# Scores of two attention pieces in one TensorE burst, five PSUM banks as one stock, and the first third in fixed sequences

## The chip, the cores and the metric

The kernel runs on one core of a Trainium2 chip. The time is that of the device from start to end, in microseconds. Engines: PE (TensorE, matrix products), DVE (VectorE), ACT (ScalarE), POOL (GpSimd) and SP, whose queue issues nearly all DMAs. PE writes its results to PSUM, which has eight banks of 128 x 512 f32.

## The reference

Attention with two kinds of masks, and behind it one feed-forward layer over all tokens. q and k are scaled by 7.3, so the scores are not small; all is f32.

```python
B, H, S, D = 8, 8, 576, 64                     # q, k, v: (B, H, S, D)
scores = q @ k.T / sqrt(D)
mask   = (0 <= i - j < 32)                     # heads 0 to 3, "local"
mask   = (i >= j) and (i % 32 == j % 32)       # heads 4 to 7, "strided"
attn   = softmax(where(mask, scores, -1e9))
x      = (attn @ v).transpose(0, 2, 1, 3).reshape(4608, 512)
h      = x @ w_in                              # 512 -> 2048
g      = h * erf(softplus(h))
out    = g @ w_out                             # 2048 -> 512
```

## The kernel before

**Feed-forward.** The 4608 tokens go in 12 chunks of 384, the 2048 hidden units in 16 slices of 128. One slice of one chunk is an f-tile; there are 192. An f-tile is a first-product group on PE (`mm1`, L814: twelve products of 128 x 384 into one PSUM bank, `h`; x and the weights are each split into a high and a low part, and three of the four combinations are summed), nine steps on ACT and DVE (L822, L819, L843, L846, L849: four tanh and products that stand for h * erf(softplus(h)), then the split into `ghi` and `glo`), and three second-product groups (`mm2`, L877: three products of 128 x 512 for each of three token tiles, summed over the slices in the banks `o0` to `o2`). The bank of `h` is free when `glo` is written. `a`, `ghi` and `glo` have two buffers each.

**Attention.** Each batch has six pieces: three thirds of the queries for the local heads (True) and three for the strided ones (False). The 12 pieces of batches 0 and 1, needed by the first chunks, are done by `head` with masks added on PE. The other 36 are done by `quad`: 32 score products of 64 x 64 (L559) into two banks (`ps`), then for each bank the mask on DVE (L574, a minimum, which also copies to SBUF and so frees the bank), the maximum on POOL (L580), subtraction on DVE (L587), exponential on ACT (L594) and the sum on POOL (L600), then DVE steps that bring the reciprocal sums into place. Two pieces share one `products` step: 64 value products (L665) into two `ps` banks, which are scaled in place (L696) and split into `xhi` (L717, ACT) and `xlo` (L722, DVE); with `xlo` the bank is free. A burst is a run of such 64 x 64 products between the 128 x 128 products of the f-tiles.

**PSUM before.** Three banks for `h` (pool `ps_h`, also for the transposes and some scores of the heads), two for `ps`, three for `o`.

**Weights.** 32 blocks of w_in and w_out come as pairs of 32-bit words (L760), are turned into f32 by three DVE steps (L766, L773, L779), and split by ACT and DVE (L784, L787). All that falls in the first third, where the loads of 16.8 MB of words, the heads and the first chunks compete.

**Order.** A planner (`Plan`) simulates the engines with a cost for each operation and picks, engine by engine, the ready operation of the smallest key; its result is the program order of each engine. Keys come from tables (`WK`, `HK`, `GK`, `AK`, `FT` ...) and, for the 1087 operations that it names, from the list `ORDER`. Ahead of the first f-tile, the planner fills PE's free time with products that nobody reads (`warm`, L1057).

The lines around which the change turns:

```python
s = [buf("ps_ps", "ps", [P, 512], f"s{i}_{pid}") for i in range(2)]     # quad
ph = buf("ps_h", "h", [P, 512], f"h_{k}")                               # ftile
px = [buf("ps_ps", "ps", [P, 512], f"x{p}_...") for p in range(2)]      # products
o_s = add("pe", 0.75, key, scores, [lq, *o_con, *last], [*s, *sm], [qk])
```

Of the kernel before, what the change touches and what calls it, by code (L numbers as in the profile page):

```python
# [32 lines left out]
WK = (-129.247, -1893.58, 98.5168, -2129.18, 127.551, 563.302, -1058.31, 207.105, 1224.65, 1267.83, 776.969, 2769.39, 1905.64, 459.073, 1076.72, 1052.12, -571.504, 270.885, -541.703, 359.21, 614.965, 583.382, 626.232, 272.891, 1466.2, 1009.72, -1281.88, 2826.45, 1224.64, 459.156, 1917.17, -1415.81)  # L33
LD = (226.738, 72.4203, -180.254)
HD = (-336.803, 299.919, 1136.27, 1085.87, -1250.39, 1255.86, -283.893, -2829.06, -1852.42, -715.65, -833.303, -831.384)
HK = (-211.98, -3338.2, -1501.79, -1392.83, 143.38, -60.2353, 220.878, 315.727, 281.824, 331.969, 646.928, 824.11)
GK = (69.7483, 204.571, -202.002, -12.5924, 109.465, 414.462, 58.9581, 1.10569, -170.147, -56.9842, 70.5204, -218.953, 0.416193, 310.64, 101.626, 128.829, -366.195, -122.429, 227.847, 32.916, 114.694, -116.251, -133.254, 189.13, 397.368, -138.217, 135.932, -37.9147, -43.0676, 44.7781, 229.201, 144.855, -268.989, -169.213, 72.314, 185.886)
QD = (-79.5815, -82.8971, -2.37199, 155.063, -3.45178)
ADT = -0.840127
CK = 40.0  # L40
AK = (77.4271, 192.803, -60.2978, 41.0326, 70.3192, 185.174, -70.7401, 2.22243, -109.704, 315.813, -26.4327, -155.795, 62.5451, 236.782, 72.0876, 265.805, 176.553, 8.32189)
PF = 26.1751
# [32 lines left out]
class Buf:  # L75


    def __init__(self, tag, make):
        self.tag, self.make, self.users = tag, make, []
        self.tile = None  # L80
# [29 lines left out]


class Op:
    def __init__(self, eng, dur, key, emit, after, new, use, earliest):
        self.eng, self.dur, self.key, self.emit, self.earliest = eng, dur, key, emit, earliest
        self.after, self.new = list(after), list(new)
        self.start = self.end = None
        self.behind = []
        self.locks = eng == "pool" or eng == "dve" and emit.__name__ in TWO
        for b in self.new + list(use):
            b.users.append(self)  # L120


class Plan:

    ENGINES = ("pe", "act", "dve", "pool", "sp")
    SAME = {"pe": 0.0, "act": 0.14, "dve": 0.13, "pool": 0.1, "sp": 0.0}
    LATENCY = {"pe": 0.25, "act": 0.2, "dve": 0.15, "pool": 0.6, "sp": 0.1}  # L130
    PATIENCE = 0.002
    ENTER = 0.08
# [12 lines left out]
    def _ready(self, op, live):  # L145
        t = op.earliest
        if any(p.end is None for p in op.behind):
            return None
        for p in op.after:
            if p.end is None:  # L150
                return None
            t = max(t, p.end + (self.SAME if p.eng == op.eng else self.LATENCY)[op.eng])
        for i, b in enumerate(op.new):
            order = live.setdefault(b.tag, [])
            n = len(order) - self.bufs[b.tag] + sum(x.tag == b.tag for x in op.new[:i])
            if n >= 0:
                for u in order[n].users:
                    if u.end is None:
                        return None
                    t = max(t, u.end + (self.SAME if u.eng == op.eng else self.LATENCY)[op.eng])  # L160
        return t

    def order(self):
        queue = {e: sorted((o for o in self.ops if o.eng == e), key=lambda o: o.key) for e in self.ENGINES}
        free = dict.fromkeys(self.ENGINES, 0.0)
        live, dma, left = {}, self.RAMP[0], len(self.ops)
        cold = None
        held = {"dve": 0.0, "pool": 0.0}
        entered = False
        while left:  # L170
            best = None
            for e in self.ENGINES:
                can = [(o, n, self._ready(o, live)) for n, o in enumerate(queue[e][: self.WINDOW])]
                floor = max(free[e], dma - BACKLOG) if e == "sp" else free[e]
                port = held.get({"dve": "pool", "pool": "dve"}.get(e), 0.0)
                can = [(max(t, floor, port if o.locks else 0.0), o.key, e, n) for o, n, t in can if t is not None]
                if e == "pe" and self.filler and self.filler[0].end is not None:
                    can.append((max(free[e], self.filler[0].end + 0.2), 1e9, e, -1))
                if can:
                    soon = min(can)[0] + self.PATIENCE  # L180
                    c = min((key, t, e, n) for t, key, e, n in can if t <= soon)
                    if best is None or c[1] < best[0]:
                        best = (c[1], c[0], c[2], c[3])
# [3 lines left out]
            if n < 0:  # L187
                o = Op(e, 0.11, 0.0, self.filler[1], (), (), (self.filler[2],), 0.0)
                self.ops.append(o)
                left += 1  # L190
            else:
                o = queue[e].pop(n)
            if self.filler and o is self.filler[3]:
                self.filler = None
            o.start = t
            if e == "sp":
                free[e] = t + 0.6
                was, dma = dma, max(dma, t + 0.6) + o.dur
                dma += self.RAMP[1] if was < 3.0 <= dma else 0.0
                o.end = dma + 1.5  # L200
# [18 lines left out]
def attention_moe(  # L219
# [58 lines left out]
    def dve(n, x=1.0):  # L278
        return 0.067 + n * x / 960.0
# [935 lines left out]
```

## Time and profile before

| | us |
|---|---|
| runs shown, median (lowest to highest) of 3 | 918.6 (918.18 to 918.61) |
| profiled execution | 918.11 |
| its span, first to last instruction | 916.3 |
| PE, DVE, ACT, POOL busy | 906.4, 691.9, 574.4, 317.4 |
| PE's share of the chain that ended last | 81% |

A busy engine is one that has an instruction in flight; the products of PE overlap, so its busy time contains what one product waits for the one before. The price of a piece of PE's work is therefore read from start to start in the timeline. Idle time is what ends a wait that nothing covered. What is off the chain costs nothing as long as it stays covered.

### The profile page before, as it was taken

To read this page: it belongs to the slowest core of one execution; us is meant where nothing else is said; L and a number is where in the kernel's file an instruction comes from. 1 tells how busy PE (TensorE), PEld (TensorE's weight loads), DVE (VectorE), ACT (ScalarE), POOL (GpSimd) and SP (SyncE) were. 2 spreads that over 40 slices of the span, in tenths; PEclk is the share of its full clock that TensorE was granted. 3 is DMA by queue.
4 is the path that set the end of the run, shared out by engine and by line. 5 is a ranking of instruction groups with operands and counts; after the bars stand their busy time and mean duration, and the time that the engine had idled before them with its cause. 6 is when DMAs were issued, how large, how long until landed. Compare 5 with 4: busy or idle time off the path is not lost.

```text
span 916.3 us, 18195 instructions
## 1 busy us (share of the span) xinstructions
PE 906.4 (99%) x7066; PEld 805.6 (88%) x7066; DVE 691.9 (76%) x1507; ACT 574.4 (63%) x1291; POOL 317.4 (35%) x170
## 2 busy tenths in 40 slices
PE   9999999999999999999999999999999999999998
PEld 6888989998888888899888888888899888999997
DVE  6999999757978888856887876788875767575553
ACT  5777677656556666566666566566656656655654
POOL 4521011304457445404455641644650323030000
PEclk9999999999999999999999999999999999999999
DMA  9972121013322122102221211212200300000000
GB/s 364 403 298 95 47 75 47 12 35 99 116 76 75 39 62 79 44 1 74 65 64 59 62 38 32 91 41 64 80 19 1 97 1 24 35 2 1 35 1 35
DMA packets 26726, 66.11 MB, mean 72 GB/s; under 512 B 2960, under 2 KB 3728, under 8 KB 26640
## 3 DMA queue, kind: packets, MB, share of 16 engines
q1 hardware_dynamic: 26496, 64.73, 20.5%
q8 instruction: 55, 0.90, 0.4%
q14 instruction: 31, 0.25, 0.1%
q10 hardware_dynamic: 144, 0.23, 0.1%
HBM read 53.15 MB, written 11.80 MB: 71 GB/s over the span
## 4 chain that ended last, share of the span: by engine, by line
PE 81%; DVE 11%; POOL 3%; ACT 2%; issue 2%; DMA 0%; SPq 0%; DVEq 0%; POOLq 0%; ACTq 0%
PE h L814 37%; PE o L877 36%; DVE a L819 2%; PE ps L559 2%; POOL su_True L600 2%; PE ps L665 1%; ACT a L822 1%; PE warm L1057 1%; POOL su_False L600 1%; DVE glo L849 1%; DVE ps L696 1%; PE av L450 1%; DVE h L843 1%; DVE xlo L722 1%; DVE sm L367 1%
## 5 line engine op out<-in xcount | busy, mean ns | idle before, releaser
L877 PE MATMUL o<-pair,ghi 128*128 128x512 f32 x1154 | 359.1, 392 | 0.0
L822 ACT ACTIVATE a<-a 128x384 f32<-128x384 f32 x576 | 294.0, 523 | 103.2 <-DVE a L819 96.9
L819 DVE SCALAR_TENSOR_TENSOR a<-a,h 128x384 f32<-128x384 f32 x384 | 209.8, 547 | 135.0 <-ACT a L822 132.1
L814 PE MATMUL h<-xhi,pair 128*128 128x384 f32 x1536 | 302.7, 339 | 2.2 <-DVE glo L849 1.8
L814 PEld LDWEIGHTS h<-xhi,pair 128*128 128x128 f32 x1536 | 268.6, 188 | 14.5 <-DVE glo L849 5.9
L877 PEld LDWEIGHTS o<-pair,ghi 128*128 128x128 f32 x1154 | 212.4, 188 | 36.4
L877 PE MATMUL o<-pair,glo 128*128 128x512 f32 x577 | 224.6, 389 | 0.0
L822 ACT ACTIVATE a<-h 128x384 f32<-128x384 f32 x192 | 94.2, 491 | 142.1 <-PE h L814 141.4
L814 PE MATMUL h<-xlo,pair 128*128 128x384 f32 x768 | 164.4, 336 | 0.0
L843 DVE TENSOR_TENSOR h<-a,h 128x384 f32<-128x384 f32 x192 | 106.4, 556 | 44.2 <-ACT a L822 43.4
L814 PEld LDWEIGHTS h<-xlo,pair 128*128 128x128 f32 x768 | 136.0, 188 | 0.0
L877 PEld LDWEIGHTS o<-pair,glo 128*128 128x128 f32 x577 | 108.3, 188 | 23.1
L580 POOL PARTITION_ALL_REDUCE mx_False<-sm_False x36 | 51.5, 1466 | 203.8 <-DVE sm_False L574 190.9
L849 DVE TENSOR_TENSOR glo<-h,ghi 128x384 fp32r<-128x384 f32 x192 | 105.2, 548 | 11.4 <-ACT ghi L846 7.9
L580 POOL PARTITION_ALL_REDUCE mx_True<-sm_True x36 | 51.5, 1467 | 175.5 <-DVE sm_True L574 137.2
L846 ACT CAST ghi<-h 128x384 fp32r<-128x384 f32 x192 | 90.9, 473 | 33.4 <-PE o L877 27.9
L600 POOL PARTITION_ALL_REDUCE su_True<-sm_True x36 | 90.5, 2552 | 49.7 <-ACT ob L919 33.6
L600 POOL PARTITION_ALL_REDUCE su_False<-sm_False x36 | 91.1, 2562 | 11.0 <-ACT a L822 2.4
L360 POOL PARTITION_ALL_REDUCE mx<-sm x22 | 34.7, 1584 | 58.5 <-DVE w L766 21.3
L717 ACT CAST xhi<-ps 128x128 fp32r<-128x128 f32 (+3 forms) x72 | 21.4, 321 | 17.5 <-DVE ps L696 13.7
L594 ACT ACTIVATE sm_False<-sm_False 128x432 f32<-128x432 f32 (+1 forms) x36 | 18.7, 524 | 12.5 <-DVE sm_False L587 12.3
L610 DVE STREAM_TRANSPOSE tt_False<-su_False 64x448 f32<-64x448 f32 (+1 forms) x36 | 21.0, 583 | 5.2 <-POOL su_False L600 2.4
(83 smaller groups left out, 617.9 us busy)
## 6 DMA issues: line engine op xcount, KB each, us to landing
out<-ob SPq DMA_DIRECT2D x35, 256.0 KB, 2.0
words<-w_in SPq DMA_DIRECT2D x16, 512.0 KB, 7.9
words<-w_out SPq DMA_DIRECT2D x16, 512.0 KB, 7.5
qk_True<-qk_loc SPq DMA_DIRECT2D x18, 416.0 KB, 3.2
qk_False<-qk_str SPq DMA_DIRECT2D x12, 472.0 KB, 3.2
v_True<-v_all SPq DMA_DIRECT2D x18, 260.0 KB, 3.7
v_False<-v_all SPq DMA_DIRECT2D x18, 260.0 KB, 3.5
v<-v_all SPq DMA_DIRECT2D x10, 260.0 KB, 7.6
```

Source lines behind the costliest of these rows:

```text
L360: yield nc.gpsimd.partition_all_reduce(mx[:, :cols], sm[k][:, :cols], P, ReduceOp.max)
L580: yield nc.gpsimd.partition_all_reduce(mx[k][:, :cols], sm[k][:, :cols], P, ReduceOp.max)
L600: yield nc.gpsimd.partition_all_reduce(su[k][:, :cols], sm[k][:, :cols], P, ReduceOp.add)
L610: yield nc.vector.transpose(tt[rows, :width], t[rows, :width])
L717: yield nc.scalar.copy(hi, src)
L814: yield nc.tensor.matmul(ph[:, :CH], win[4 * s + cc][:, w, fs], x[cc // 2][:, cc % 2, c0 : c0 + CH], start=(i == 0), stop=(i == len(terms) ...
L819: yield nc.vector.scalar_tensor_tensor(out=out, in0=in0, scalar=scalar, in1=in1, op0=op0, op1=op1)
L822: yield nc.scalar.activation(dst, src, func, bias=bias[i], scale=scale)
L843: yield nc.vector.tensor_tensor(out=ph[:, :CH], in0=a.tile, in1=ph[:, :CH], op=ALU.mult)
L846: yield nc.scalar.copy(ghi.tile, ph[:, :CH])
L849: yield nc.vector.tensor_tensor(out=glo.tile, in0=ph[:, :CH], in1=ghi.tile.bitcast(F32), op=ALU.subtract)
L877: yield nc.tensor.matmul(po[:, half], g[:, ts], wout[f][:, w, half], start=(f == fs0 and i == 0), stop=(f == fs1 and i == 2 and half.stop ...
```

## The change

1. `quad` no longer issues its scores. A new function `attend` takes two pieces and issues their 64 score products as one PE step, which needs the four score banks of both at once; `softmax` holds the steps behind it as they were. There are 18 such bursts instead of 36.
2. The pools `ps_h` and `ps_ps` become one stock of five banks for `h`, score, value and transpose tiles. The planner picks the bank that has been free longest, and a step starts in its plan only when as many banks as it needs are vacant. Five banks are cleared at the start instead of two.
3. In the plan, score and value steps are put 0.5 us behind the moment at which they could start (`SLACK`), and the costs of loads are changed (first data at 3.05 us, 395 GB/s, landing 0.8 us).
4. Operations named in `ORDER` keep exactly that sequence on their engine (`strict`), SP's excepted; so do all first-product groups and score bursts. `ORDER` has new contents and names 1400 operations instead of 1087, up to about the 60th f-tile; the other tables of keys are new too.

```diff
-LD = (226.738, 72.4203, -180.254)
+LD = (-455.947, -13.8716, -393.415)
-QD = (-79.5815, -82.8971, -2.37199, 155.063, -3.45178)
+QD = (-172.068, -5.26238, -82.1718, 124.272, 198.844)
...
+SHARED, NBANK = {"ps", "s", "t", "h"}, 5
...
-    RAMP = 0.9, 1.4
+    BEGIN, LANDING = 3.05, 0.8
+    SLACK = {"scores": 0.5, "av": 0.5, "mm1": 0.0}
...
-        return t
+        need = sum(b.tag in SHARED for b in op.new)
+        if need:
+            free = sorted(self._vacant(op.eng))
+            if len(free) < need:
+                return None
+            t = max(t, free[need - 1][0])
+        return t + op.slack
+
+    def _vacant(self, eng):
+        out = []
+        for n, b in enumerate(self.held):
+            if b is None:
+                out.append((0.0, n))
+            elif all(u.end is not None for u in b.users):
+                out.append((max(u.end + (self.SAME if u.eng == eng else self.LATENCY)[eng] for u in b.users), n))
+        return out
...
-                can = [(o, n, self._ready(o, live)) for n, o in enumerate(queue[e][: self.WINDOW])]
+                can = [(o, n, self._ready(o, live)) for n, o in enumerate(queue[e][: self.WINDOW]) if not o.strict or o is turn[e][0]]
...
+            vacant = sorted(self._vacant(o.eng)) if any(b.tag in SHARED for b in o.new) else []
             for b in o.new:
                 live[b.tag].append(b)
+                if b.tag in SHARED:
+                    b.bank = vacant.pop(0)[1]
+                    self.held[b.bank] = b
...
-    banks = [ps_a.tile([P, 512], F32, name=f"ps{i}") for i in range(2)]
+    banks = [ps_a.tile([P, 512], F32, name=f"ps{i}") for i in range(NBANK)]
...
-        o_s = add("pe", 0.75, key, scores, [lq, *o_con, *last], [*s, *sm], [qk])
-        o_s.behind.extend(order_t)
...
+    def attend(pair, key, dt, last):
+
+        def scores():
+            for g in pair:
+                yield from g.scores()
+
+        o_s = plan.add(
+            "pe", 1.21, key, scores, [g.lq for g in pair] + [*o_con, *last],
+            [x for g in pair for x in (*g.s, *g.sm)], [g.qk for g in pair],
+        )
+        o_s.behind.extend(order_t)
+        o_s.slack, o_s.strict = plan.SLACK["scores"], True
+        for m, g in enumerate(pair):
+            softmax(g, o_s, key + 0.3 * m, dt)
+        return o_s
...
-        ph = buf("ps_h", "h", [P, 512], f"h_{k}")
+        ph = buf("ps", "h", [P, 512], f"h_{k}")
...
-    for i in range(2):
-        z = buf("ps_ps", "ps", [P, 512], f"clear{i}")
-        plan.add("dve", 0.4, -20.0 + i, clear(z), [], [z])
+    for i in range(NBANK):
+        z = buf("ps", "ps" if i < 4 else "s", [P, 512], f"clear{i}")
+        plan.add("dve", 0.4, -20.0 + 0.1 * i, clear(z), [], [z])
...
     for n, i in enumerate(ORDER):
         plan.ops[i].key = n - 10000.0
+        plan.ops[i].strict |= plan.ops[i].eng != "sp"
```

The order on PE, in the seventh chunk, before: the scores of the second and third strided piece of batch 5 (`qk_5_False_1`, `qk_5_False_2`; `o0_6` is a bank of the chunk's output, `h_101` the bank of f-tile 101). Sixteen rows stand for the 32 products of a piece, twelve for a first-product group.

```order
L877 MATMUL o0_6_0_5974<-pair17_311,ghi_97_5978 128x512 x2
L877 MATMUL o0_6_0_5974<-pair17_311,glo_97_5987 128x512
L559 MATMUL ps1_90<-qk_5_False_1_5734 64x54
L559 MATMUL ps0_89<-qk_5_False_1_5734 64x54
...
L814 MATMUL h_101_6093<-xhi0_81,pair4_1163 128x384
...
L559 MATMUL ps1_90<-qk_5_False_2_5778 64x36
L559 MATMUL ps0_89<-qk_5_False_2_5778 64x36
...
L877 MATMUL o1_6_0_5981<-pair17_311,ghi_97_5978 128x512 x2
```

The same two pieces on PE now; `ps0` to `ps4` are the five banks of the stock.

```order
L923 MATMUL o0_6_0_5762<-pair24_1554,ghi_104_6121 128x512 x2
L923 MATMUL o0_6_0_5762<-pair24_1554,glo_104_6129 128x512
L582 MATMUL ps3_89<-qk_5_False_1_5850 64x54
L582 MATMUL ps4_90<-qk_5_False_1_5850 64x54
...
L582 MATMUL ps2_88<-qk_5_False_2_5865 64x36
L582 MATMUL ps0_86<-qk_5_False_2_5865 64x36
...
L923 MATMUL o1_6_0_5771<-pair24_1554,ghi_104_6121 128x512 x2
...
L858 MATMUL ps1_87<-xhi0_78,pair8_1679 128x384
...
L858 MATMUL ps3_89<-xhi0_78,pair8_1679 128x384
...
L858 MATMUL ps4_90<-xhi0_78,pair12_1233 128x384
```

The two score bursts, which had a first-product group between them, are one that takes four banks; one second-product group and three first-product groups follow, into the fifth bank and into two banks of the burst.

The start of DVE's order before (`cap`, `con`, `ident` and `neg` are constants, `w32_2` is weight block 2).

```order
L1060 MEMSET cap_86 128x150
L974 MEMSET ps0_89 128x512
L974 MEMSET ps1_90 128x512
L959 CAST con_85<-con_f_91 128x446
L960 COPY ident_88<-con_f_91 128x128
L963 TENSOR_SCALAR neg_87<-con_f_91 128x128
```

The start of DVE's order now, and further down the fourth clear with its neighbours.

```order
L1106 MEMSET cap_83 128x150
L1005 CAST con_82<-con_f_91 128x446
L1006 COPY ident_85<-con_f_91 128x128
L1020 MEMSET ps0_86 128x512
L1020 MEMSET ps1_87 128x512
L1009 TENSOR_SCALAR neg_84<-con_f_91 128x128
...
L1020 MEMSET ps4_90 128x512
...
L1020 MEMSET ps3_89 128x512
```

The clears have moved behind the constants, three stand in the first ten rows, and two are among the work of the heads.

## Rows read from the trace of the kernel before

**Rows 1.** The page: span, busy times by engine, shares of the chain by engine.
```profile
span 916.3 us, 18195 instructions
PE 906.4 (99%) x7066; PEld 805.6 (88%) x7066; DVE 691.9 (76%) x1507; ACT 574.4 (63%) x1291; POOL 317.4 (35%) x170
PE 81%; DVE 11%; POOL 3%; ACT 2%; issue 2%; DMA 0%; SPq 0%; DVEq 0%; POOLq 0%; ACTq 0%
```
**Rows 2.** Busy time by stretch: length, five engines, granted clock, DMA share, GB/s.
```profile
0.00:25.00 25.00, 23.00 (x268) 17.37 (x269) 15.89 (x34) 14.12 (x37) 11.19 (x11) 1.00 0.95 366
25.00:50.00 25.00, 25.00 (x288) 21.68 (x286) 24.12 (x57) 18.71 (x58) 13.37 (x9) 1.00 1.03 405
...
45.60:107.40 61.80, 60.47 (x442) 54.28 (x441) 60.69 (x142) 43.74 (x95) 12.45 (x9) 1.00 0.45 164
107.40:912.70 805.30, 802.33 (x6102) 716.63 (x6101) 595.12 (x1288) 500.06 (x1108) 282.52 (x144) 1.00 0.15 47
331.00:359.10 28.10, 27.82 (x256) 24.54 (x255) 22.39 (x52) 18.12 (x43) 15.66 (x8) 1.00 0.25 78
```
**Rows 3.** The chain that ended last, in order of time: start, length, what.
```profile
6.57 2.51 PE warm L1057 x23
...
885.96 4.17 PE h L814 x24
890.12 4.08 PE o L877 x18
...
904.53 8.21 PE o L877 x39
```
**Rows 4.** Timeline of PE: start, length, line, operation, out<-in, count, [idle].
```profile
209.44 1.16 PE L665 MATMUL ps<-sm_True,v_True 64*64 64x64 f32 x64
210.53 1.67 PE L814 MATMUL h<-xhi,pair 128*128 128x384 f32 x8
...
303.45 1.55 PE L814 MATMUL h<-xhi,pair 128*128 128x384 f32 x8
...
305.63 0.69 PE L559 MATMUL ps<-qk_False 64*64 64x54 f32 x32
306.24 1.67 PE L814 MATMUL h<-xhi,pair 128*128 128x384 f32 x8
...
308.54 0.67 PE L559 MATMUL ps<-qk_False 64*64 64x36 f32 x32
309.14 0.73 PE L877 MATMUL o<-pair,ghi 128*128 128x512 f32 x2
...
313.35 1.55 PE L814 MATMUL h<-xhi,pair 128*128 128x384 f32 x8
```
**Rows 5.** Waits of PE's weight loads from 100 us on: total, times, longest.
```profile
PEld h L814 <- DVE glo L849: 5.2, 12, 0.7
PEld ps L559 <- DVE xlo L722: 4.3, 9, 0.8
```
**Rows 6.** Timeline of DVE, ACT and PE at the start and around the first f-tile.
```profile
1.11 1.03 DVE L974 MEMSET ps<- 128x512 f32 x2
...
39.67 0.68 DVE L787 TENSOR_TENSOR pair<-w,pair 128x512 fp32r<-128x512 f32 x1
...
44.23 0.26 ACT L389 CAST xhi<-t 128x144 fp32r<-128x144 f32 x1
...
44.52 0.31 DVE L394 TENSOR_TENSOR xlo<-t,xhi 128x144 fp32r<-128x144 f32 x1 [0.29 <-ACT xhi L389]
...
45.60 1.65 PE L814 MATMUL h<-xhi,pair 128*128 128x384 f32 x8
47.09 0.86 PE L814 MATMUL h<-xlo,pair 128*128 128x384 f32 x4
...
52.98 0.76 PE L328 MATMUL ps<-qk 128*128 128x144 f32 x4 [0.87 <-DVE xn L476]
```
**Rows 7.** Groups by line: the mask, count, busy time, mean ns, idle before.
```profile
L574 DVE TENSOR_TENSOR sm_True<-ps,cap 128x384 f32<-128x384 f32 x36 | 18.5, 549 | 0.5 <-PE ps L559 0.2
```

More of the change, by code (lines that the diff above doesn't have):

```diff
@@ L79, in __init__ @@
         self.tag, self.make, self.users = tag, make, []
-        self.tile = None
+        self.tile = self.bank = None
     def __getitem__(self, key):
@@ L169, in order @@
         entered = False
+        turn = {e: [o for o in queue[e] if o.strict] for e in self.ENGINES}
         while left:
@@ L240, in attention_moe @@
     ps_a = ctx.enter_context(tc.tile_pool(name="ps_a", bufs=1, space=PSUM))
-    ps_h = ctx.enter_context(tc.tile_pool(name="ps_h", bufs=3, space=PSUM))
     ps_o = ctx.enter_context(tc.tile_pool(name="ps_o", bufs=1, space=PSUM))
@@ L282, in act, with group @@
         return fixed + n / 1200.0
-    def group(b, loc, j, bank="ps", spare=None):
+    def group(b, loc, j, spare=None):
         g = SimpleNamespace()
@@ L305, in group @@
             sm, sm_b = [Part(both, i) for i in range(nbank)], [both]
-        s = [buf("ps_" + bank, bank, [P, 512], f"s{i}_{pid}") for i in range(nbank)]
-        pt = buf("ps_h", "h", [P, 512], f"t_{pid}")
+        s = [buf("ps", "s", [P, 512], f"s{i}_{pid}") for i in range(nbank)]
+        pt = buf("ps", "t", [P, 512], f"t_{pid}")
         def place(i, blk, h):
@@ L404, in loads, with head @@
         return lq, lv
-    def head(b, loc, j, key, dt, early, bank, num, sub_pe_too, norm_act):
+    def head(b, loc, j, key, dt, early, num, sub_pe_too, norm_act):
         spare = num if num < 6 else None
-        g = group(b, loc, j, bank, spare)
+        g = group(b, loc, j, spare)
         sm_b = g.sm_b
@@ L415, in head @@
         mx = [Part(mx_b, i) for i in range(nbank)]
-        pav = [buf("ps_o" if early else "ps_ps", f"o{i}" if early else "ps", [P, 512], f"av{i}_{pid}") for i in range(2)]
+        pav = [buf("ps_o" if early else "ps", f"o{i}" if early else "ps", [P, 512], f"av{i}_{pid}") for i in range(2)]
         xn_b = [buf("apool", "tt", [P, 512], f"xn{i}_{pid}") for i in range(2)]
@@ L535, in quad @@
         v = buf("zpool", "v", [P, 2 * WV], f"v_{pid}")
-        s = [buf("ps_ps", "ps", [P, 512], f"s{i}_{pid}") for i in range(2)]
+        s = [buf("ps", "ps", [P, 512], f"s{i}_{pid}") for i in range(2)]
         sm = [buf("apool", "sm", [P, 512], f"sm{i}_{pid}") for i in range(2)]
@@ L633, in quad, with softmax @@
         order_q[:], order_v[:] = [lq], [lv]
-        o_s = add("pe", 0.75, key, scores, [lq, *o_con, *last], [*s, *sm], [qk])
-        o_s.behind.extend(order_t)
+        done = [[], []]
+        return SimpleNamespace(**{k: x for k, x in locals().items() if k != "add"})
+    def softmax(g, o_s, key, dt):
+        s, sm, mx, su, tt, rc, cols, width = g.s, g.sm, g.mx, g.su, g.tt, g.rc, g.cols, g.width
+        mask, maxi, sub, exp, total, gather, invert, spread = g.mask, g.maxi, g.sub, g.exp, g.total, g.gather, g.invert, g.spread
+        add = plan.add
         o_e = []
@@ L857, in ftile @@
         first = add("pe", 2.08, v0, mm1, ready[0] + mm1_first[-1:], [ph])
+        first.strict = True
+        first.slack = plan.SLACK["mm1"] if pos else 0.0
         o = add("act", tp, at(FT[0]), n1, [first], [a], [ph])
@@ L1025, in chunks_of @@
         return [1] if (loc and j == 0) else ([2] if loc else [1, 2])
-    quads = []
+    quads, last = [], []
     for b in range(B):
@@ L1032, in attention_moe @@
                 n = 6 * b + i
-                done = head(b, loc, j, HK[n], HD[n], b == 0, "ps" if b or i % 2 else "h", n, SUB_PE[n], NORM_ACT[n])
+                done = head(b, loc, j, HK[n], HD[n], b == 0, n, SUB_PE[n], NORM_ACT[n])
                 for c in to:
@@ L1037, in attention_moe @@
                 k = 6 * b + i - 12
-                a = quad(
-                    b, loc, j, PRO + SLOT * GK[k], ADT * SLOT, PRO + SLOT * AK[k // 2] + k % 2, [quads[-1][0].o_s] if quads else []
-                )
+                a = quad(b, loc, j, PRO + SLOT * AK[k // 2] + 0.1 * (k % 2))
                 quads.append((a, b // 2, to))
                 if k % 2:
-                    products((quads[-2][0], quads[-1][0]), PRO + SLOT * AK[k // 2], ADT * SLOT)
+                    pair = (quads[-2][0], a)
+                    last = [attend(pair, PRO + SLOT * GK[k // 2], ADT * SLOT, last)]
+                    products(pair, PRO + SLOT * AK[k // 2], ADT * SLOT)
     for a, p2, to in quads:
```

58 lines of the change are left out of this document (30 added, 28 removed).

## The prediction, made before the changed kernel ran

> **What bounds the kernel now.** I read the page's totals first, then the busy times by stretch, then the chain that ended last, then TensorE's timeline at single places and the waits. The profiled execution took 918.11 us, of which 916.3 us are the span; the median of the three runs shown is 918.6 us, 0.5 us above. The sum below is made against 918.11. PE is busy 906.4 us of the span and carries 81% of the chain; DVE has 11% of it [rows 1]. By stretch, DVE is full from 25 to 107 us (24.12 of 25.00 and 60.69 of 61.80 us), and the DMA engines are full up to 50 us. After that PE is full: from 107.40 to 912.70 us it is idle for 805.30 - 802.33 = 3.0 us, at granted clock 1.00, while DVE has 210 us to spare [rows 2]. So a gain must come from work that PE no longer does, from PE's waits, or from the start before the first f-tile at 45.60 us [rows 6].
>
> What PE does behind 107.40 us can be counted. Where nothing disturbs it, 24 first products take 4.17 us, that is 2.08 us per f-tile, and 18 second products 4.08 us, that is 0.68 us per token tile and 2.04 us per f-tile [rows 3]. By the order of before, 180 first-product groups (375 us) and 545 second-product groups (371 us) stand behind this point, with 36 score bursts of 0.62 us and 18 value bursts of 1.09 us (42 us) [rows 4]. Together 788 us. The stretch has 805.3, so 17.5 us are something else: the price of going in and out of a burst, and waits.
>
> The price of a burst can be read where none waits. A first-product group ahead of a burst starts it after 305.63 - 303.45 = 2.18 us instead of 2.08; the group between two bursts takes 308.54 - 306.24 = 2.30 us; the six second products behind take 313.35 - 309.14 = 4.21 us instead of 4.08 [rows 4]. So two bursts cost 0.10 + 0.22 + 0.13 = 0.45 us beside their own products, 0.22 us each. I use 0.21. Fifty-four bursts make 11.3 us. What is left, some 6 us, are waits: 3.0 us of visible idle time and what PE loses when it starts up again. By name they are waits for glo (a bank of h that is not yet free) and for xlo (a bank of ps that is not yet free) [rows 5].
>
> **The change part by part.**
>
> Scores of two pieces in one burst. The order shows 18 score bursts of 64 products in place of 36 of 32, with the same products. Eighteen entries and exits go: 18 x 0.21 = **-3.8 us**. No row of before shows two pieces' scores back to back, so the seam between them is bounded: at 0.21 us the merge saves nothing, at 0 it saves all. The nearest row is the value burst, which runs the 64 products of two pieces in 210.53 - 209.44 = 1.09 us, 17 ns each [rows 4], with no seam of that size. I take 0.
>
> Five banks as one stock. Before, h has three banks and attention two; now a paired burst takes four of the five at once, so at most one f-tile may hold a bank when it starts. The order puts a long run of second products ahead of each burst and three first-product groups behind it. The first of the three uses the fifth bank, the next two use banks of the burst, and they need them only after two groups of work (0.68 and 2.08 us). DVE frees a bank with one mask of 0.55 us [rows 7], and the first piece's masks can run during the second piece's products, so this is covered unless DVE comes 1.5 us late. If that cover is gone, PE waits at the second or third group. In a dense stretch the order gives an f-tile some nine us of other PE work between its two products, so a late glo hurts less than before. What the burst waits for is the release of the last f-tiles' banks and of the two banks of the value products of the pair before: glo and xlo, the waits of rows 5. Before, the bursts' weight loads stood 4.3 us for xlo in nine places, at most 0.8 us; the first products' loads 5.2 us for glo in twelve [rows 5]. The planner now leaves 0.5 us ahead of every score and value burst, about the mean of these nine waits (0.48). Ends: all 6 us of waits go (-6), or every one of the 18 bursts stands 0.8 us (14.4 - 4.3 = +10). Behind a waiting burst stand three first products, and behind these ACT and DVE run dry, so such a wait is not made up. I take **-2 us**, about half of the waits on xlo.
>
> DVE's share of this: the pieces' operations are the same in number. A dense stretch of before, with one pair and six f-tiles, has DVE busy 22.39 of 28.10 us and GpSimd 15.66 [rows 2]. The new order's densest stretches also have six f-tiles from burst to burst. DVE stays under PE there; its queue is in order, so single hold-ups of one 0.55 us operation remain possible.
>
> The first third in fixed sequences. All engines get new orders up to about the 60th f-tile; what can cost or give more than a wait lies at the start, where DVE and the DMAs are full. PE's fillers ahead of the first f-tile fall from 135 to 123; 23 of them take 2.51 us, 0.109 us each [rows 3], so twelve are 1.3 us. This counts only if the data come earlier too. The data of the first group in before: the last xhi piece ends at 44.23 + 0.26 = 44.49 us, its xlo at 44.83, and the group starts at 45.60 us and reads xlo 1.49 us later [rows 6]. So there are 1.1 us of margin on xhi. Against it: five clears of banks on DVE instead of two, 0.52 us each [rows 6]. Three stand in the first ten rows, where DVE is idle 9.1 of 25 us [rows 2]; the two others fall where DVE is full and add 1.0 us ahead of the first group's last operand. The first group also needs the second weight block (w1), which DVE finished at 39.67 + 0.68 = 40.35 us in before [rows 6]. On SP's queue one weight block and one q/k piece more and one v piece less stand ahead of it now, 0.67 MB, 1.7 us at 405 GB/s [rows 2], and on DVE's queue some 4 us more work (an estimate: its order's operations by their mean times); so it is ready at about 44.2 us, where 45.60 - 1.3 = 44.3 would want it. Ends: -1.3 and +1.0. I take **-0.7 us**: the margin of 1.1 us carries the clears, and what is missing for the full 1.3 I leave out, since both operands come only just in time. Behind the first group the order interrupts the f-tiles for head work 13 times instead of 11, 2 x 0.2 = **+0.4 us**. The tail behind the last second product, which ends at 904.53 + 8.21 = 912.74 us [rows 3], has the same operations as before.
>
> Sum: 918.1 - 3.8 - 2.0 - 0.7 + 0.4 = **912.0 us**.
>
> **The rivals.**
>
> First: the start does not give, and the waits stay. DVE fills the stretch from 25 to 107 us [rows 2], the two clears and the shifted weights delay the first f-tile by 1.0 us, and bank waits of the new kind replace the old ones one for one. 918.1 - 3.8 + 1.0 + 0.4 = 915.7 us. For it: DVE is the bound there. Against it: the margin of 1.1 us [rows 6].
>
> Second: the waits go altogether, since the f-tiles have nine or more us between their two products where a tile's own chain is nine steps on ACT and DVE of about the 0.55 us of rows 7, some 5 us. 918.1 - 3.8 - 6 - 0.7 + 0.4 = 908.0 us. Against it: with two ghi and two glo buffers a tile's last steps still wait for second products two tiles before.
>
> Third, on the other side: the burst's four banks. In a dense stretch the chain of a pair (four masks, eight GpSimd reductions that keep it busy 15.66 of 28.10 us [rows 2], then gather, scale, hi, lo) ends shortly before the next burst needs its banks. Before, a burst needed two banks, now four at once, and it comes once instead of in two parts. If each of the 18 bursts stands 0.8 us, the longest that rows 5 shows, the time is 918.1 - 3.8 - 0.7 + 0.4 + 10.1 = 924 us. It decides from (3.4 + 0.7 + 4.3) / 18 = 0.47 us per burst on, where the gains are used up. Against it: the planner's 0.5 us of margin, and that such waits now come up in nine places of 36 only.
>
> Fourth: the price of a burst is paid per piece and not per burst, so that the merge saves nothing: 912.0 + 3.8 = 915.8 us. Against it: the value bursts [rows 4].
>
> Fifth: PE's waits become regular and its clock falls to the lower level, 1.2 GHz, in the dense stretches. Ten f-tiles at half speed would cost 41 us, 953 us. Against it: the granted clock is 1.00 in every stretch of rows 2, also in the one with PE's longest idle time behind the start, 0.87 us at 52.98 us [rows 6]. The Trainium skill, "TensorE: Matmul & The Clock Gate", section "A second HAM failure mode: psum-queue depth-cycling", tells of a kernel that cycled through PSUM banks and idled PE between groups of products, so that the clock swung between its two levels; a shared stock of banks is the place for it. By that rule this rival would decide; the trace of before, with two small stocks that are cycled as hard, shows no such swing.
>
> **How the numbers follow.** Forecast 912.0 with its own range of 909.5 to 915: 0.58. First rival 0.14, second 0.12, third 0.10, fourth 0.05, fifth 0.01. Two runs of this kernel can be told apart from about 0.2% (1.8 us) on: faster is below 916.8 here, slower above 920.4. Faster: 0.58 + 0.12, most of the first (0.10) and 0.02 of the fourth: 0.82. Slower: most of the third (0.08) and the fifth: 0.09. The same: the rest, 0.09. The range of 8 in 10 leaves out the deepest part of the second case and most of the third: 907.5 to 918.
>
> **What would show it.** Right: 18 score bursts of about 1.25 us, each with one surcharge; the first first-product group before 45.6 us; PE's waits on xlo and glo behind 107 us smaller in sum; granted clock 1.00. The stretch behind the first f-tile shorter by 4 to 6 us. Wrong: score bursts that wait for xlo or glo in most of 18 places, a seam inside the burst, a first f-tile after 46 us, or PE idle for more than the 61.80 - 60.47 = 1.3 us of before between 45.60 and 107.40 us [rows 2].

## The result and the profile after

The changed kernel takes 909.62 us (median of 4 runs, 909.1 to 910.02) against 918.51 us for the kernel before on the same chip (4 runs, 918.18 to 918.61): a ratio of 0.9904 with a 95% interval of 0.9886 to 0.9921. The forecast was 912.0 us, with 907.5 to 918.0 as its range. The profiled execution has a span of 907.4 us, 8.9 us less than the 916.3 of [rows 1].

First the page after, with the span, the busy times and the shares of the chain, which answer to [rows 1]:

```profile
span 907.4 us, 18181 instructions
PE 898.5 (99%) x7054; PEld 803.1 (89%) x7054; DVE 687.2 (76%) x1510; ACT 571.9 (63%) x1291; POOL 317.6 (35%) x170
PE 92%; DVE 4%; DMA 2%; ACT 1%; issue 1%; POOL 0%; ACTq 0%; DVEq 0%; POOLq 0%
```

Of the 8.9 us, 906.4 - 898.5 = 7.9 are gone from PE's busy time itself, and the share of DVE in the chain has fallen from 11 to 4%. The stretches, with the columns of [rows 2], cut at the first f-tile and at the last second product of this kernel:

```profile
25.00:50.00 25.00, 24.96 (x284) 21.34 (x283) 23.76 (x61) 19.73 (x59) 12.23 (x9) 1.00 1.03 404
45.07:107.40 62.33, 61.03 (x448) 54.78 (x447) 60.39 (x146) 44.60 (x96) 12.32 (x9) 1.00 0.46 166
107.40:903.70 796.30, 793.96 (x6097) 714.68 (x6095) 590.49 (x1285) 496.45 (x1106) 282.26 (x144) 1.00 0.14 47
```

The granted clock is 1.00 throughout, as before. PE is idle for 62.33 - 61.03 = 1.3 us behind the first f-tile, as before, and for 796.30 - 793.96 = 2.3 us in the rest, where [rows 2] had 3.0. So visible idle time has given 0.7 us. TensorE's timeline shows the rest, at the first f-tile and at one merged burst (start, length, line, operation, out<-in, count; L858 and L923 are the first and second products, L582 the scores):

```profile
45.08 1.65 PE L858 MATMUL ps<-xhi,pair 128*128 128x384 f32 x8
...
298.97 0.73 PE L923 MATMUL o<-pair,ghi 128*128 128x512 f32 x2
300.09 0.50 PE L923 MATMUL o<-pair,glo 128*128 128x512 f32 x1 [0.39 <-DVE glo L893]
300.52 1.14 PE L582 MATMUL ps<-qk_False 64*64 64x54 f32 x64
301.59 0.73 PE L923 MATMUL o<-pair,ghi 128*128 128x512 f32 x2
```

The first f-tile starts 0.5 us earlier than in [rows 6]. The merged burst lasts 301.59 - 300.52 = 1.07 us, where two single ones took about 0.61 us each [rows 4]. Over all 18 bursts the mean from start to start is 1.084 us. Of the 36 before, 31 take 0.619 on average; behind the other five the next product waits, 1.7 us in all. So a merged burst is about 0.16 us shorter inside than two that it replaces, besides the entry and exit that are gone.

The waits of the weight loads for `glo` from 100 us on, which answer to [rows 5] (in all, times, longest):

```profile
PEld ps L858 <- DVE glo L893: 3.2, 6, 1.1
PEld o L923 <- DVE glo L893: 0.8, 1, 0.8
```

The 4.3 us for xlo ahead of score bursts are gone, and the waits for glo have fallen from 5.2 to 3.2 us. But they stand in few and long places.

Where the gain came from can be summed from TensorE's records, each group of products taken from its start to the start of the next, less its undisturbed duration [rows 3]. By that sum the last second product ends 9.0 us earlier:

- the start, 0.5;
- inside the score bursts, 36 x 0.619 - 18 x 1.084 = 2.8;
- beside the score bursts, 18 entries and exits at the 0.21 of the prediction, 3.8;
- waits behind 107 us, that is what is left there besides the products and 0.21 for each burst, 1.8 (5.7 to 3.9 us);
- the work of the heads, 0.1: its groups are 1.75 us shorter (13.49 to 11.74), but the f-tile products around them take 1.6 us more beyond their undisturbed durations (2.05 to 3.66).

A later kernel in which hardly a wait is left behind 107 us (noadd_free) bears out the 0.21: the products beside its 36 bursts take 7.8 us more than undisturbed, 0.22 for each burst. Most of the 1.6 us is a new wait ahead of the scores of a head group. Here a load of q and k ends it; in four other executions with the same start a DVE step of the heads does:

```profile
61.98 0.69 PE L366 MATMUL ps<-qk 64*64 64x64 f32 x32 [0.98 <-DMA qk<-qk_loc]
```

### The profile page after: what moved, and what is told of

Read it like the earlier page. It is cut to its first block, busy times and chain, and to the rows that moved or that the text cites. A ratio compares the mean times of both kernels' runs of the same rounds, so it can differ in the third digit from the quotient of the medians.

```text
span 907.4 us, 18181 instructions
## 1 busy us (share of the span) xinstructions
PE 898.5 (99%) x7054; PEld 803.1 (89%) x7054; DVE 687.2 (76%) x1510; ACT 571.9 (63%) x1291; POOL 317.6 (35%) x170
## 4 chain that ended last, share of the span: by engine, by line
PE 92%; DVE 4%; DMA 2%; ACT 1%; issue 1%; POOL 0%; ACTq 0%; DVEq 0%; POOLq 0%
PE ps L858 42%; PE o L923 41%; PE ps L582 2%; PE ps L708 2%; DVE a L863 1%; PE warm L1103 1%; PE ps L461 1%; PE av L473 1%; DMA qk<-qk_loc 1%; ACT a L866 1%; PE ps L366 1%; PE ps L473 1%; DMA con_f<-consts 0%; DMA part<-ob 0%; PE ps L449 0%
## 5 line engine op out<-in xcount | busy, mean ns | idle before, releaser
L923 PE MATMUL o<-pair,ghi 128*128 128x512 f32 x1154 | 359.1, 392 | 0.6 <-DVE ob L968 0.6
L863 DVE SCALAR_TENSOR_TENSOR a<-a,ps 128x384 f32<-128x384 f32 x384 | 209.8, 548 | 126.8 <-ACT a L866 122.9
L858 PE MATMUL ps<-xhi,pair 128*128 128x384 f32 x1536 | 300.9, 338 | 1.6 <-DVE glo L893 1.6
L858 PEld LDWEIGHTS ps<-xhi,pair 128*128 128x128 f32 x1536 | 269.5, 188 | 12.0 <-DVE glo L893 3.9
L923 PEld LDWEIGHTS o<-pair,ghi 128*128 128x128 f32 x1154 | 212.5, 188 | 38.1 <-ACT sm_False L617 1.0
L923 PE MATMUL o<-pair,glo 128*128 128x512 f32 x577 | 224.6, 389 | 0.4 <-DVE glo L893 0.4
L866 ACT ACTIVATE a<-ps 128x384 f32<-128x384 f32 x192 | 94.4, 492 | 152.4 <-PE ps L858 151.8
L858 PE MATMUL ps<-xlo,pair 128*128 128x384 f32 x768 | 164.4, 336 | 0.0
L887 DVE TENSOR_TENSOR ps<-a,ps 128x384 f32<-128x384 f32 x192 | 106.4, 554 | 40.0 <-ACT a L866 39.5
L858 PEld LDWEIGHTS ps<-xlo,pair 128*128 128x128 f32 x768 | 136.0, 188 | 0.0
L923 PEld LDWEIGHTS o<-pair,glo 128*128 128x128 f32 x577 | 108.3, 188 | 23.8 <-DVE glo L893 0.8
L893 DVE TENSOR_TENSOR glo<-ps,ghi 128x384 fp32r<-128x384 f32 x192 | 105.3, 549 | 25.0 <-ACT ghi L890 21.5
L890 ACT CAST ghi<-ps 128x384 fp32r<-128x384 f32 x192 | 91.5, 477 | 46.1 <-PE o L923 24.8
L965 ACT COPY ob<-o 128x512 f32<-128x512 f32 x35 | 20.0, 587 | 8.4 <-DMA out<-ob 2.9
```

Source lines behind the costliest of these rows:

```text
L858: yield nc.tensor.matmul(ph[:, :CH], win[4 * s + cc][:, w, fs], x[cc // 2][:, cc % 2, c0 : c0 + CH], start=(i == 0), stop=(i == len(terms) ...
L863: yield nc.vector.scalar_tensor_tensor(out=out, in0=in0, scalar=scalar, in1=in1, op0=op0, op1=op1)
L866: yield nc.scalar.activation(dst, src, func, bias=bias[i], scale=scale)
L887: yield nc.vector.tensor_tensor(out=ph[:, :CH], in0=a.tile, in1=ph[:, :CH], op=ALU.mult)
L890: yield nc.scalar.copy(ghi.tile, ph[:, :CH])
L893: yield nc.vector.tensor_tensor(out=glo.tile, in0=ph[:, :CH], in1=ghi.tile.bitcast(F32), op=ALU.subtract)
```

## The experiments

Theory 1: the gain is mostly the 18 bursts fewer, at 0.37 us each, 0.21 beside the burst and 0.16 inside. Rival 1: only the 0.21 beside. Rival 2: the gain belongs to the new order and the common stock of banks. All ratios are against the kernel before on the same chip; differences from the changed kernel are taken to its median of 909.64 us.

**The changed kernel again**, as the measure for the next three.

> The changed kernel once more, as the measure for the other runs of this chip: 909.6 us, 0.990 of the kernel before.

909.64 us (909.34 to 910.42), ratio 0.9903, interval 0.9888 to 0.9918.

**The merge undone on TensorE alone.** In the loop that issues the plan:

```diff
+    rest = None
...
-        for ins in op.emit():
+        it = iter(op.emit())
+        if op.emit.__qualname__.endswith("attend.<locals>.scores"):
+            for _ in range(32 // 2):
+                tc.keep_in_program_order(next(it))
+            rest = [it, 2 - 1]
+            continue
...
+        for ins in it:
             tc.keep_in_program_order(ins)
...
+            if op.eng == "pe" and rest:
+                for _ in range(32 // 2):
+                    tc.keep_in_program_order(next(rest[0]))
+                rest[1] -= 1
+                rest = rest if rest[1] else None
```

> The changed kernel with its 18 merged score bursts cut in two again: one 128-row product of the second-product or first-product group that follows is issued between the two pieces, so that TensorE switches 18 times more; the plan, the banks, the sequences and every other instruction stay. Theory 1 (the merge pays, 0.21 us beside a burst and 0.16 us inside it): 18 x 0.37 = 6.7 us longer, 916.3 us, and a score burst in the trace back at 0.62 us per piece. Rival 1 (only the surcharge beside a burst, as the prediction had it): 18 x 0.21 = 3.8 us, 913.4 us. Rival 2 (the gain is that of the new order and of the common stock of banks): unchanged, 909.6 us.

917.23 us (915.97 to 917.55), ratio 0.9978, interval 0.9969 to 0.9987: 7.6 us of the 8.8 are gone. TensorE's timeline of this kernel at the same burst:

```profile
303.30 0.69 PE L582 MATMUL ps<-qk_False 64*64 64x54 f32 x32
303.92 0.50 PE L923 MATMUL o<-pair,ghi 128*128 128x512 f32 x1
304.35 0.67 PE L582 MATMUL ps<-qk_False 64*64 64x36 f32 x32
304.95 0.50 PE L923 MATMUL o<-pair,ghi 128*128 128x512 f32 x1
```

The first piece takes 303.92 - 303.30 = 0.62 us again, and the single product between the pieces holds TensorE for 304.35 - 303.92 = 0.43 us, where a product among its like takes 0.68 / 3 = 0.23: 0.20 us for one exit and one entry. By the same sum over groups as above, 18 x (0.15 + 0.21) = 6.5 us are price; the rest, 1.1 us by the medians, is longer waits. So in the changed plan rival 1 (3.8) and rival 2 (0) fall: this kernel keeps the new order, the sequences and the common stock, and 918.41 - 917.23 = 1.2 us of the gain are left to it.

**The burst in four**, the same edit with quarters of eight products. Each of these products is two records in the profile; the 64 and 32 products of a burst in [rows 4] and in the text above are such records.

> The changed kernel with each merged score burst cut in four, one 128-row product between the quarters: 54 switches more than in the changed kernel. Theory 1: 54 x 0.37 = 20 us longer, 929.6 us. Rival 1: 54 x 0.21 = 11.3 us, 920.9 us. Rival 2: unchanged. If the price inside a burst belongs to the pieces (64 products of one piece share nothing with those of the other) and not to the switch, this kernel stands 3 x 0.21 x 18 = 11.3 us above the changed one and the first cut 0.37 x 18.

930.51 us (929.85 to 931.29), ratio 1.0128, interval 1.0114 to 1.0142: 20.9 us above the changed kernel, 0.39 us for each of the 54 switches. The price belongs to the switch and not to the piece, since cuts inside one piece cost the same.

```profile
305.78 0.45 PE L582 MATMUL ps<-qk_False 64*64 64x54 f32 x16
306.17 0.50 PE L923 MATMUL o<-pair,ghi 128*128 128x512 f32 x1
306.60 0.45 PE L582 MATMUL ps<-qk_False 64*64 64x54 f32 x16
306.98 0.50 PE L923 MATMUL o<-pair,ghi 128*128 128x512 f32 x1
```

16 records take 0.39 us, 32 take 0.62 and 64 take 1.08. These lie on a straight line: about 0.16 us once, and 14.4 ns for each record.

**The value bursts cut in two**, the same edit on the attention-value products.

> The changed kernel with its 18 bursts of attention-value products cut in two, one 128-row product between the two pieces. If the price belongs to the change between 64-row and 128-row products and not to the scores, it is the same as for the scores: 18 x 0.37 = 6.7 us, 916.3 us; if it belongs to the scores alone, 909.6 us.

914.48 us (913.39 to 915.3), ratio 0.9953, interval 0.9941 to 0.9966: 4.8 us longer and not 6.7. The price is there: by the sum over groups the bursts take 2.8 us more inside and some 3.3 us beside. But the waits fell by 0.3 to 0.5 us in each of five long places. One of the five is the wait at 61.98 us, ahead of all value bursts, which is of another length in each execution (0.5 to 1.2 us of idle time). That DVE, which frees the banks, had more time at the other four is likely and not shown. So the price is that of the scores, and what it adds to the time depends on whether TensorE would have waited anyway.

**The first third without its fixed sequences.** The order table stays as priorities:

```diff
     for n, i in enumerate(ORDER):
         plan.ops[i].key = n - 10000.0
-        plan.ops[i].strict |= plan.ops[i].eng != "sp"
+        pass
```

> The changed kernel, its order table kept as priorities, but without the rule that the first third is issued in that sequence; merged bursts and the common stock of five banks stay. Theory 1 (nearly all of the gain is the 18 bursts fewer): the price of the bursts stays saved, and at most what the start and the head groups gave goes, 0.5 + 1.75 us: 909.6 to 912 us. Rival 2 (new order and stock of banks): nearly the whole gain goes, 916 us or more, with the waits of TensorE up by 6 us.

919.43 us (918.7 to 920.86), ratio 1.0012, interval 1.0003 to 1.0021. For this kernel the forecast of theory 1 was wrong and that of rival 2 right: with 18 merged bursts still in place the whole gain is gone. TensorE's timeline ahead of its first f-tile:

```profile
45.08 1.91 PE L1103 MATMUL warm<-cap 128*128 128x256 bf16 x16
46.83 0.29 PE L508 MATMUL ps<-ident,xn 72*128 72x72 f32 x2
46.95 2.46 PE L1103 MATMUL warm<-cap 128*128 128x256 bf16 x21
49.17 1.65 PE L858 MATMUL ps<-xhi,pair 128*128 128x384 f32 x8
```

The first f-tile comes 4.1 us later, behind 37 fillers; the head groups take 14.68 us behind it instead of 11.74, the products around them 0.4 us less, and the waits behind 107 us 3.0 us more: 4.1 + 2.9 - 0.4 + 3.0 = 9.6 us at the last second product. The bursts themselves take 1.083 us, as in the changed kernel. That does not make the sequences worth 9.8 us over the kernel before, which had a table of priorities made for its own plan: the new plan loses this without them. What merged bursts would be worth in the plan of before, and what the common stock, the 0.5 us of slack or the new load costs would be worth by themselves, no run shows.

**What the switch is.** Three products in each merged burst, after its first three quarters, write to unused columns of a score bank; four kernels differ in the product:

```diff
-            for g in pair:
-                yield from g.scores()
+            for m, g in enumerate(pair):
+                for n, ins in enumerate(g.scores()):
+                    yield ins
+                    if n not in ((7, 15), (7,))[m]:
+                        continue
+                    yield nc.tensor.matmul(out, lhs, rhs, start=True, stop=True, skip_group_check=True)
```

```
kernel  out                     lhs                      rhs                     product
same    g.s[0][:64, 432:512]    g.qk[:64, :64]           g.qk[:64, :80]          64 rows, f32
kind    g.s[0][:64, 432:512]    win[0][:64, 0, :64]      win[0][:64, 0, :80]     64 rows, fp32r
mode    g.s[0][:, 432:512]      g.qk[:, :P]              g.qk[:, :80]            128 rows, f32
both    g.s[0][:, 432:512]      win[0][:, 0, :P]         win[0][:, 0, :80]       128 rows, fp32r
```

> The changed kernel with three products put into each merged score burst, after each quarter but the last: 128 rows by 128 columns, plain f32 as the scores, 80 columns written to unused columns of a score bank. It changes the rows of the array (64 to 128) and not the number format. Theory A (the price of a burst is that of going between 64-row and 128-row products): 54 x 0.37 = 20 us and some 54 x 0.1 for the products themselves, 935 us. Theory B (the price is that of going between f32 and fp32r): the products alone, 5 us, 915 us.

> The same places, with a 64-row by 64-column product in fp32r: it changes the number format and not the rows of the array. Theory A: the products alone, 54 x 0.03, 911 us. Theory B: 20 us more, 931 us.

> The same places, with a 128-row by 128-column product in fp32r of 80 columns: both change, as between a score burst and its neighbours. Theories A and B alike: 20 us and 54 x 0.04 for the products, 932 us.

> The control of the three kernels with products put into the merged score bursts: at the same places a 64-row by 64-column product of 80 columns in plain f32, as the scores around it, so that neither rows nor number format change (the three took 28.4, 19.3 and 21.5 us over the changed kernel). Theory C (either change alone stops the overlap of neighbouring products and costs some 0.3 us or more): 54 x 0.03 to 0.06 us, 911 to 913 us. Theory D (any product that is foreign to the burst costs this, by its place in the array or its bank, whatever its kind): 929 us or more.

Measured: mode 938.06 us (ratio 1.0215, interval 1.02 to 1.0231), kind 928.97 (1.0112, 1.0098 to 1.0126), both 931.16 (1.0138, 1.0124 to 1.0152), same 917.67 (0.9986, 0.9977 to 0.9996). Over the changed kernel 28.4, 19.3, 21.5 and 8.0 us. TensorE's timeline at one place each, first kind, then both, then mode (L690 is the added product):

```profile
304.57 0.45 PE L582 MATMUL ps<-qk_False 64*64 64x54 f32 x16
304.95 0.25 PE L690 MATMUL ps<-pair 64*64 64x80 f32 x1
305.13 0.45 PE L582 MATMUL ps<-qk_False 64*64 64x54 f32 x16
```

```profile
305.58 0.45 PE L582 MATMUL ps<-qk_False 64*64 64x54 f32 x16
305.97 0.30 PE L690 MATMUL ps<-pair 128*128 128x80 f32 x1
306.20 0.45 PE L582 MATMUL ps<-qk_False 64*64 64x54 f32 x16
```

```profile
307.06 0.45 PE L582 MATMUL ps<-qk_False 64*64 64x54 f32 x16
307.44 0.45 PE L690 MATMUL ps<-qk_False 128*128 128x80 f32 x2
307.82 0.45 PE L582 MATMUL ps<-qk_False 64*64 64x54 f32 x16
```

In each the quarter takes 0.38 to 0.39 us up to the product's start, as in the burst cut in four, instead of the 1.08 / 4 = 0.27 of a quarter inside a merged burst. In the kernel "same" it does not:

```profile
303.54 0.45 PE L582 MATMUL ps<-qk_False 64*64 64x54 f32 x16
303.81 0.24 PE L690 MATMUL ps<-qk_False 64*64 64x80 f32 x1
303.82 0.27 PE L582 MATMUL ps<-qk_False 64*64 64x54 f32 x3
```

There the next score product starts 0.01 us behind the added one. Within the bursts, without what later waits add, one added product costs 0.13 us (same), 0.33 (kind), 0.39 (both) and 0.53 (mode). Neither A nor B holds: a change of the number format alone costs 0.2 us more than a product of the burst's own kind, a change of the rows alone 0.4, part of which is the longer product itself (its two records start 0.17 us apart). The product of the kernel "kind" also reads another operand, a block of w_in in place of q and k, which no run separates from its format. Theory C comes nearest, though its 0.03 to 0.06 us for the control was too low. How the 0.37 us of a burst divide between the two changes stays open, since both together cost hardly more than the format alone.

**The waits that were left.** PE's two longest visible idle times behind 107 us are at 516 and 706 us, 0.66 and 0.65 us. DVE's, GpSimd's and TensorE's timelines of the changed kernel at the first of them:

```profile
510.53 0.58 DVE L633 STREAM_TRANSPOSE tt_True<-su_True 64x384 f32<-64x384 f32 x1
511.14 1.13 DVE L639 TENSOR_SCALAR r_True<-tt_True 128x12 f32<-128x12 f32 x1
512.31 0.23 DVE L643 RECIPROCAL r_True<-r_True 128x12 f32<-128x12 f32 x1
...
515.73 0.51 DVE L893 TENSOR_TENSOR glo<-ps,ghi 128x384 fp32r<-128x384 f32 x1
```

```profile
510.29 2.86 POOL L623 PARTITION_ALL_REDUCE su_False<-sm_False  x1
```

```profile
515.25 0.39 PE L923 MATMUL o<-pair,glo 128*128 128x512 f32 x1
516.29 1.66 PE L858 MATMUL ps<-xhi,pair 128*128 128x384 f32 x8 [0.66 <-DVE glo L893]
```

The two products start 516.29 - 515.25 = 1.04 us apart instead of 0.23, so the place costs 0.8 us where 0.66 show as idle. The one that waits does so for `glo`, which DVE writes last of the steps shown. TENSOR_SCALAR adds 1e-9 to 9 to 14 columns of sums, 12 here. Its durations over the kernel, for the local and the strided pieces (minimum, median, maximum in ns):

```profile
L639 DVE TENSOR_SCALAR r_True<-tt_True x18: 161/174/1134, 169.2 to 804.3; 128x12 f32<-128x12 f32 x18
L639 DVE TENSOR_SCALAR r_False<-tt_False x18: 161/167/460, 222.8 to 764.2; 128x14 f32<-128x14 f32 x12, 128x9 f32<-128x9 f32 x6
```

At 169, 217, 377, 421 and 472 us no reduction runs on GpSimd, and it takes 0.16 to 0.17 us. Where it takes 0.46 us or more, GpSimd is inside a reduction: at 344, 371, 646 and 798 us it ends 1.77 to 1.78 us after that reduction's start, and at 511 and 701 us 1.98 us after it. Only the 0.50 us at 291 fall late in a reduction and end 0.03 us behind its end. DVE's queue behind the addition stands still, and with it the steps that free a bank for the first products. The edit, and a second kernel with the last two lines as well, in which GpSimd does not wait for the reciprocal:

```diff
-            yield nc.vector.tensor_scalar(
-                out=rc[:, :nb, 0], in0=tt[:, :width].rearrange("p (c k) -> p c k", k=32)[:, :, 0],
-                scalar1=1e-9, scalar2=None, op0=ALU.add,
-            )
-            yield nc.vector.reciprocal(rc[:, :nb], rc[:, :nb])
+            yield nc.vector.reciprocal(rc[:, :nb, 0], tt[:, :width].rearrange("p (c k) -> p c k", k=32)[:, :, 0])
...
-        if op.eng == "dve" and (op.locks or op.emit.__name__ == "invert"):
+        if op.eng == "dve" and (op.locks or op.emit.__name__ == "invert" and "quad" not in op.emit.__qualname__):
```

> The changed kernel without the one VectorE instruction that adds 1e-9 to the sums of the late attention pieces (the sums hold exp(0) = 1, so that the addition changes no bit), 36 instructions fewer. Theory on the waits left: the two longest (0.66 us at 516 and 0.65 us at 706) come from that instruction, which took 1.13 us there and 0.17 us where GpSimd was idle; without it VectorE is 0.9 us earlier at both, and 0.3 to 0.4 us at 291 and 797: 1.5 to 2.5 us shorter, 907.1 to 908.1 us. Rival (TensorE waits there for the bank because five banks are too few, whatever VectorE does): same, 909.6 us. A second rival: the reciprocal behind it takes over the stall (0.23 us before, about 1 us then), same time.

> As the kernel without the addition, and GpSimd's next reduction no longer waits for the reciprocal of the late pieces. If the reciprocal needs nothing that GpSimd holds: as the kernel before it or up to 0.5 us shorter; if it does, the stall comes back on it and the time is that of the changed kernel, 909.6 us.

906.02 us (905.31 to 906.65), ratio 0.9863, interval 0.9848 to 0.9879; with GpSimd freed as well 905.97 us, 0.9864 (0.9851 to 0.9878), which is the same: the reciprocal takes 0.20 to 0.25 us there too, beside a reduction or not. Both are faster than the kernel before and the changed one. Against the changed kernel the first is 3.6 us shorter by the medians and 2.9 by the spans of the profiled executions, more than the 1.5 to 2.5 expected. DVE and TensorE at the same place, without the addition:

```profile
510.09 0.57 DVE L633 STREAM_TRANSPOSE tt_True<-su_True 64x384 f32<-64x384 f32 x1
510.70 0.23 DVE L639 RECIPROCAL r_True<-tt_True 128x12 f32<-128x12 f32 x1
510.96 0.58 DVE L643 STREAM_TRANSPOSE tt_True<-r_True 128x384 f32<-128x384 f32 x1
```

```profile
514.36 0.62 PE L919 MATMUL o<-pair,ghi 128*128 128x512 f32 x2
514.81 0.39 PE L919 MATMUL o<-pair,glo 128*128 128x512 f32 x1
515.04 1.55 PE L854 MATMUL ps<-xhi,pair 128*128 128x384 f32 x8
```

The reciprocal takes 0.23 us beside the same reduction, which runs from 509.84 us on here, and the first product follows the second ones without a wait. So neither the stock of five banks nor the reciprocal held TensorE there; the addition did. No run keeps an instruction of 0.17 us in its place, so how much of the 3.6 us is the stall, and how much the chain that is one instruction shorter, is not separated. From 107 us on PE is idle for 1.1 us in this kernel:

```profile
107.40:900.95 793.55, 792.49 (x6096) 715.08 (x6094) 583.14 (x1248) 495.77 (x1106) 282.10 (x144) 1.00 0.14 48
```

**The same in the kernel before.**

> The kernel before the change without the instruction that adds 1e-9 to the sums of the late pieces. It took 1.35 us at 520.67 and 1.25 us at 622.07 there too, 0.6 us in three more places. If the stall cost the kernel before as much as the changed one (3.6 us), 914.8 us; if the looser order of before hid it, 917 us or more.

915.57 us (915.18 to 915.85), ratio 0.9968, interval 0.9956 to 0.9981: 2.7 us shorter. The addition was in the kernel before too and cost it nearly as much; its stall is no consequence of the change.

## Why the prediction was right, term by term

The forecast of 912.0 us was 2.4 us too high, with the right sign. The merged bursts are its largest term, as they turned out to be, but with the wrong size; the reason behind the second term was incomplete.

- **The bursts, -3.8 us.** Mis-sized: the price is 0.37 us and not 0.21, and 18 of them make 6.6 us. The prediction counted what a burst costs its neighbours and took its inside as proportional to its products ("score bursts of about 1.25 us"). They take 1.084. [Rows 4] already held it: the 64 value products take 1.09 us there, the two score bursts of 32 take 306.24 - 305.63 = 0.61 and 309.14 - 308.54 = 0.60, together 0.12 more. I read that row only as a sign that there is no seam. The cut bursts show about 0.16 us once per burst and 14.4 ns per record. This is also why the stretch behind the first f-tile is 8.5 us shorter and not the 4 to 6 that were named as a sign.
- **The waits, -2 us.** Measured about -1.8 behind 107 us. That the size came out is in part luck: it was a choice between -6 and +10. The waits on xlo went, as the prediction had it, but others came in their place, rarer and longer. What it had incomplete was to lay all waits to the stocks of banks. The bank was only what TensorE waited for; what delayed it at its two longest idle times was an addition of 0.17 us that stood for 1.13 us beside GpSimd's reduction. Without the addition the waits behind 107 us fall from 3.9 to 1.3 us in the changed kernel, and from 5.7 to 2.5 in the kernel before, whose banks are as they were. The waits' names in [rows 5] gave the last step of that chain, and I did not follow DVE's queue further back.
- **The start, -0.7 us.** Measured -0.5: 45.60 to 45.08 us. These are single executions: in ten more with the same start the first f-tile begins at 45.08 to 45.62 us, and in one more with the start of before (before_noadd) at 46.34. The fixed sequences carry it: without them it begins at 49.17 us.
- **Two more interruptions, +0.4 us.** They are there, but the work of the heads as a whole became 0.1 us shorter. The groups themselves lost 1.75 us, for which the prediction had no term; in [rows 6] the wait of 0.87 us at 52.98 was half of it, and it is gone. The new wait of 0.98 us at 61.98 took more than half of that back.
- **The rivals.** The first (915.7) had the waits replaced one for one and a later start: some were replaced, but not all, and no profiled execution of the changed kernel starts after 46 us. A burst that waits for its four banks (924) did not come: no score burst stands for a bank any more. The price per piece (915.8) is refuted by the burst cut in four. That the waits go altogether (908.0) did not come with the change; without the addition most of them are gone. The clock stayed at the higher of its two levels, 1.00, in every stretch, so what the Trainium skill, "TensorE: Matmul & The Clock Gate", section "A second HAM failure mode: psum-queue depth-cycling", tells of did not come, although five banks were shared.

## What to carry to other kernels

Price a burst of small products by two bursts of different length, so that its fixed part inside shows beside the surcharge on its neighbours; then count switches, not products. When an engine waits for a buffer, follow the chain back through the queue of the engine that frees it until an instruction takes longer than its own median: a wait for a bank can be a stall of an unrelated instruction earlier in that queue. A new plan's order at the start can cost as much as the plan saves, so its two parts are measured one by one.

## What the runs showed of the hardware

A product of another number format is dear inside a burst as well as one of other rows. A 64-row product in fp32r among 64-row products in f32 costs 0.33 us, one in f32 at the same place 0.13, though the first is one record in the profile and the second two. Whether its other operand has a part in this is not shown. The Trainium skill, "TensorEngine Tiling (Array Packing)", section "Tiling Modes", says that changing the tiling mode drains the engine. The 0.53 us of the 128-row f32 product agree with it; the 0.33 us of the fp32r product came without such a change.

VectorE's TENSOR_SCALAR on f32 in SBUF stood, in six of its seven long places, until 1.8 to 2.0 us after the start of GpSimd's partition reduction (up to 1.13 us for an operation of 0.17), in the seventh until the reduction's end, and the RECIPROCAL put in its place does not (0.20 to 0.25 us at all 36 places). The Trainium skill, "GPSIMD Engine Reference", section "1. Specifications", says that GpSimd's SBUF interfaces are shared with VectorE, with contention against its instructions in a 2-port perf mode or with two SBUF inputs. These rows agree with it, if the addition ran in such a mode, which no row shows.
